# Fifteen block products instead of eleven for the first MLP product of the last two chunks, and last stores on two queues

## The chip, the cores and the metric

The kernel runs on one core of one Trainium2 chip. The metric is the device time of one execution in microseconds, lower is better. Before the change the median of three runs is 528.09 us (527.87 to 530.99).

## What is computed

Eight-head delta-rule attention over a sequence of 768 tokens in four batches, followed by one MLP block with a residual. The reference, cut:

```python
k_n = k / (norm(k) + 1e-6)                      # q, k, v: (4, 8, 768, 48)
for t in range(768):                            # state: (4, 8, 48, 48)
    y[t]  = q[t] @ state
    state = state + beta[t] * outer(k_n[t], v[t] - k_n[t] @ state)
x   = y with heads side by side                 # (4, 768, 384)
xn  = (x - mean) / sqrt(var + 1e-6) * g_ln
out = x + relu(xn @ w_ch1) @ w_ch2              # 384 -> 1536 -> 384
```

Everything is float32. One float32 matmul is two TensorE instructions in the profile.

## The kernel before

**Chunks.** The sequence is cut into 12 chunks of 64 tokens; with four batches a chunk is 256 tokens wide. `recur(c)` carries the delta-rule state from chunk to chunk (small matmuls into the PSUM tiles `two` and `by`, sums on DVE, copies on ACT) and ends in the layer norm. From chunk 3 on the normed tile is transposed on DVE, written to DRAM (`xld`) and read back turned, and ACT multiplies it by the gain into `xnt` (line 1377), three blocks of 128 features. Then `mlp(c)` runs: it is what fills TensorE beside the recurrence of later chunks. The recurrence is ahead of the MLPs: that of chunk 11 has ended when the MLP of chunk 10 begins.

**First product, `eleven` (line 1451).** It forms the hidden layer, 1536 x 256, from `w1_sb` as 2 x 3 blocks (768 x 128) and `xnt` as 3 x 2 blocks (128 x 128), by a scheme of eleven block products in place of twelve. A block product is 6 matmuls of 128x128 weights by 128 columns, so a chunk has 66 matmuls, 132 instructions, all at line 1492. They need sums of token blocks (`d_`, five GpSimd sums per chunk, line 1472) and sums of weight blocks, which `sums_of_w1` (line 1447) makes once, two of them in place in `w1_sb`. The block products accumulate in the four PSUM banks `f0` to `f3`; ACT (lines 1509, 1512) and DVE (lines 1515, 1528) combine them into `h_all`, in two groups with 512 and 256 columns per operation.

**Second product, `seven` (line 1642).** Seven block products of 6 matmuls with 192 columns each (line 1664), with GpSimd forming sums and differences of `h_all` (lines 1650, 1689) and DVE and GpSimd adding up the output tiles `os_` (line 1682). `put(c, g)` stores an output tile with two DMAs (line 600), one for each batch, all on SP's queue. In the last chunk `put(11, 1)` comes first and `put(11, 0)` last.

**Order.** Nothing is issued as it is written down. Each operation is handed to `Line.add` with a cost, and `Line.schedule` plays a list schedule with due times `DUE`, limits `CAP` and one offset `OFF` for each part of the program. `emit` issues in the order of planned starts, and `in_this_order` pins that order on every engine. So a change of a part, or of a number in these lists, moves instructions on all engines; each engine takes its own strictly in order, and a wait at the head holds up all that stands behind it.

Of the kernel before, what the change touches and what calls it, by code (L numbers as in the profile page):

```python
# [16 lines left out]
C = 64  # L17
DP = 64
BK = 32
# [33 lines left out]
def dve(n):  # L53
    return 0.16 + 1.04e-3 * n


def act(n):
    return 0.17 + 0.83e-3 * n
# [371 lines left out]
def kernel(  # L430
# [38 lines left out]
    FROM = 3  # L469
    TOK = 256  # L470
# [6 lines left out]
    def sb(name, shape, dt=FP32):  # L477
        return const.tile(shape, dt, name=name)
# [60 lines left out]
    d_ = [t[:, half_w + 128 * i : half_w + 128 * i + 128] for t in second for i in range(2)] + [ident]  # L539
    st = sb("st", [128, 2, 2, 6])  # L540
# [13 lines left out]
    DUE = [-305.067857599, -184.157488926, 455.196580585, 43.3608971536, 325.931658715, 418.81557092, 734.822875439, 596.087521503, 954.313194593, 1226.15149798, 1753.77174886, 1187.43924725, -1.6924469742, 7.47712706956, 1.31274637377, 1177.34078649]  # L554
    CAP = [747.889715428, 1212.19696458, 1084.81830387, 1850.25080892, 1448.91733639, 908.561376039, 705.970562755, 575.226842462, 821.351411096, 750.46942201, 1687.9172189, 1227.4281115, 847.781737921, 881.489018474, 1102.45793961, 1447.53022967, 1091.57755388]
    T0 = [32.9830988769, 43.9377940451, 29.0921020937, 44.9281472705, 63.7206388166, 107.721780452, 109.01717894, 42.4201425188, 137.327678312, 9.9371017997, 7.55135349446, 21.1072922972, 47.3695615515, 3.2653345546, 12.003557196, 58.3820362978, 9.11313409582, 34.3183793157, 80.7294725245, 31.0940483985, 65.2240956281, 73.1210354066, 26.5270080195, 53.6799046277, 66.9289646085, 120.165225966]
    OFF = [-61.6829581914, -49.2365532767, -61.5532218662, 17.9216944294, -8.93066007944, -19.7935657519, -0.868007026628, 0, 8.96654600389, -13.8380038365, -50.331393939, -0.246849623501, -27.4676130541, 7.77550058171, -22.6886143688, -3.86879544818, -821.586638896, -2.38324144815, -18.1419009006, 5.55478119707, -0.273775179226, -4.22332705522, 80.7687098368, -5.39747372829, -20.4523790178, 62.9055142488, -7.43344176114, 31.9790263038, 21.8074958819, 8.7032008021, 8.84329072182, -13.4908722439, -14.3458640854, -21.0142536144, -8.17343430205, -9.08488196034, 3.21270803936, 29.7501729987, -370.210698155, 9.64783740174, -54.0771745917, 0, 6.02876528764, -18.715620035, -0.0266946289401, -157.574112514, 0.282239804554, -7.26929256528, -11.082495992, -8.27251668698, 6.02892269239, -13.9072145046, 0.152204562562, 22.7850900002, -47.5224937959, -1.16466857269, 2.33155240109, -49.6486518684, -51.2601416133, -62.465549245, -258.793504219, 1.2326483113, 35.4487428898, 31.3088385871, 11.2699410861, -113.147994473, 15.6085619425, -5.03125681565, -202.178096924, -25.0752772067, -0.665071753919, -6.77933533358, 3.23511675889, -68.4395072164, -60.5873923385, -42.4358792875, -97.9842212258, 12.0160900273, 18.6777945201, -900.573997296, -391.422008629, -20.8554491287, 12.9662458348, 1.75202460465, -24.9412070649, 4.97794129872, 75.9129714421, 9.69658805447, 5.43644995158, -526.886362328, -23.7620747742, 4.87077107518, 20.8620167161, 22.9095302211, -1.446032994, -2.31148664706, -2.833545276, 55.9003753723, 63.1638387207, -218.31594106, 287.768221191, 39.9673797514, 0, 804.43668455, 12.7893706811, 40.0678037528, 191.615596099, 0, 7.62314549532, 0, 51.2829387214, 28.4043993347, -5.30420927608, 18.5190140875, -7.64728420003, 7.63987656771, 61.2399462693, 717.489554984, 104.850886777, -30.443334038, -17.6796729001, 1.15630637025, 33.0836625929, 44.5914396091, 124.896962022, 76.2257084997, -17.2048186859, 9.19876963592, 11.8954016929, 17.6790867831, 26.5462796852, 8.59903556167, 24.5744786777, 48.2415672492, 84.1439987925, 573.112593574, -0.31404467451, 2.58380493428, 8.06139582684, -33.4691328586, -35.9526386931, -3.41549753963, 12.8997354829, -1.70472339012, -86.5639462817, 30.2317600188, 0.770084801705, 4.89412762855, 18.4175254922, -4.62459749441, -11.6877931109, 15.5755669109, -4.74496253875, 7.29402960805, -3.92469752656, -16.6201385477, -20.5867367042, 28.2665321084, 4.92853485667, 0, 15.3621971178, -8.42832996846, -56.587083905, 4.72501651567, -56.0564350712, -36.0703739182, 29.6200097296, 32.9003356762, -13.8377451749, 27.2835896047, -1.24739066499, 8.93640941449, 3.28676443186, 297.478212758, -19.9986109974, 45.0956057028, 0, -23.0001510965, 0, 36.6024183436, -9.30579353749, 11.8322652961, 15.1603515043, -21.1764521199, -3.23342658561, 10.9691701204, 0, -53.330288128, -6.9355981517, 35.7517193679, 17.1361544279, -16.5818223692, 7.98946302238, -5.9600414049, 135.238583305, 43.2173490845, 35.7070773331, 1504.57932506, -1.37439939367, 2.80197877523, 83.3684246786, -142.866519066, -50.2056045983, 97.2746589799, 0.00958371475404, 1.62790837443, -2.01014429694, 1.24356061286, 12.6149232043, -4.38744746062, -11.0164345418, -23.3392998149, -60.6068970653, -10.8042936204, -38.5434794118, 2.00080739243, -2.74074762392, -5.2820291742, -29.0236507323, 43.1273234385, 0.946905692554, -24.3700937813, 0, -21.7407793415, -12.5188513858, -23.5560537382, -50.7954370929, -3.45193559535, 15.4383131463, -11.5511037154, 16.3023360558, -25.1832177565, 16.2211956562, 10.4191918731]
# [22 lines left out]
    def half(e):  # L580
        return slice(C * e, C * e + C)
# [837 lines left out]
    def due(c, t):  # L1419
        return DUE[c] + DUE[12 + min(c, 2)] * t  # L1420
# [9 lines left out]
    def w1_part(i, k):  # L1430
        return w1_sb[:, k, i * half_w : i * half_w + half_w], [("w1", k, i, n) for n in range(2)]
# [109 lines left out]

    def mlp(c):
# [5 lines left out]
        if c >= FROM:  # L1548
            hs = [(c * FT + f) % NH for f in range(FT)]
            if c == FROM:  # L1550
                sums_of_w1(True)
            eleven(c, hs)
            return seven(c, hs, 33 * 0.43)
# [43 lines left out]
    def o_keys(g):  # L1597
        return [("o", g, n) for n in range(2)]

    def put(c, g):  # L1600
        line.part += 1
        for e in range(2):
            dma(
                "SP", out[2 * e + g, c * C : (c + 1) * C, :], os_[g][half(e)], C, 105, o_keys(g), [("out", c, g, e)], pr=-5
            )
# [36 lines left out]
    def seven(c, hs, t1=1.3 * FT):  # L1642
# [35 lines left out]
        def sum_(eng, out_, a, b_, r, w, pr=-5):  # L1678
            e = {"Pool": nc.gpsimd, "DVE": nc.vector}[eng]
            add(  # L1680
                eng, dve(D2) if eng == "DVE" else 0.1 + 2.27e-3 * D2,
                lambda: e.tensor_tensor(out=out_, in0=a, in1=b_, op=ALU.add), r, w, pr=pr,  # L1682
            )
# [27 lines left out]
        sum_("Pool", o[1][0], o[1][0], v2, ["v2"], [("o", 1, 0)])  # L1711
# [180 lines left out]
```

## Time and profile before

| what | value |
|---|---|
| median of three runs | 528.09 us |
| profiled execution, own time | 528.0 us |
| span of the profile, first to last instruction | 526.1 us |
| PE busy | 497.6 us (95%), 9706 instructions |
| DVE / ACT / POOL busy | 369.0 / 188.2 / 212.6 us (70 / 36 / 40%) |
| DMA | 40.53 MB, mean 77 GB/s |

The own time of the profiled execution is 1.9 us more than its span; a sum made on the trace is made against 528.0 us. Busy time of PE counts a matmul until its result is there; since matmuls are pipelined, two neighbours overlap, and the distance of two starts says what one costs, not its length.

### The profile page before, as it was taken

What the parts mean: (1) busy time and instruction counts of PE and PEld (TensorE: products, weight loads), DVE (VectorE), ACT (ScalarE), POOL (GpSimd) and SP (SyncE); (2) the same over time, 40 slices, a digit from 0 to 9 for tenths busy, and PEclk for the clock granted to TensorE, in tenths of its full rate; (3) what the DMA queues carried; (4) which work ended last, traced back from release to release, by engine and by line L of the source; (5) the groups of instructions that cost most, each with busy time, mean ns of one, the idle gap of its engine ahead of it and who ended that gap; (6) DMA issues with size and microseconds to landing.
All of it is one profiled execution on the core that took longest, in us unless ns stands there. A gap on an engine that the chain in (4) does not pass through costs nothing.

```text
span 526.1 us, 22198 instructions
## 1 busy us (share of the span) xinstructions
PE 497.6 (95%) x9706; PEld 451.6 (86%) x9706; DVE 369.0 (70%) x849; ACT 188.2 (36%) x420; POOL 212.6 (40%) x320
## 2 busy tenths in 40 slices
PE   6867699999999999999999999999999999999996
PEld 3656577778898999989999889999889999999995
DVE  2899569997399866879895579895678893452321
ACT  2824855414612523525204422513523213242030
POOL 6151432246424560642724342452351815235352
PEclk8776889999999999999999999999999999999999
DMA  9975544365645444454311525121233010221101
GB/s 160 283 138 123 83 133 138 91 103 82 81 70 82 83 90 77 100 80 116 49 31 19 99 55 94 48 61 33 65 64 92 1 32 4 64 68 24 31 2 31
DMA packets 157457, 40.53 MB, mean 77 GB/s; under 512 B 150816, under 2 KB 153888, under 8 KB 157360
## 3 DMA queue, kind: packets, MB, share of 16 engines
q1 hardware_dynamic: 153520, 29.40, 31.3%
q10 hardware_dynamic: 3552, 9.63, 5.8%
q8 instruction: 76, 1.25, 1.0%
q0 software_dynamic: 288, 0.07, 0.2%
q14 instruction: 21, 0.17, 0.1%
HBM read 30.82 MB, written 8.26 MB: 74 GB/s over the span
## 4 chain that ended last, share of the span: by engine, by line
PE 85%; DVE 7%; issue 2%; DMA 2%; POOL 1%; SPq 1%; ACT 0%; DVEq 0%; ACTq 0%
PE f L1664 27%; PE f L1492 25%; PE f L1561 10%; PE two L1256 4%; PE f L1583 3%; PE two L1217 2%; PE by L1217 2%; PE by L1271 2%; PE two L1018 2%; PE two L1281 2%; PE by L1018 1%; DMA kr<-in_k_dram 1%; DVE tmp L1089 1%; PE f L1141 1%; DVE xb L1096 1%
## 5 line engine op out<-in xcount | busy, mean ns | idle before, releaser
L1650 POOL TENSOR_TENSOR h_all<-h_all 128x256 f32<-128x256 f32 x99 | 73.7, 749 | 78.1 <-PE f L1664 65.2
L1664 PE MATMUL f<-w_sb,h_all 128*128 128x192 f32 x396 | 97.2, 334 | 0.9 <-issue 0.5
L1664 PE MATMUL f<-words,h_all 128*128 128x192 f32 x396 | 90.1, 329 | 0.0
L1492 PE MATMUL f<-xnt,w_sb 128*128 128x128 f32 x648 | 87.1, 277 | 0.4 <-ACT xnt L1377 0.3
L1492 PEld LDWEIGHTS f<-xnt,w_sb 128*128 128x128 f32 x648 | 80.0, 192 | 1.6 <-ACT xnt L1377 0.9
L1664 PEld LDWEIGHTS f<-w_sb,h_all 128*128 128x128 f32 x396 | 66.3, 190 | 4.8 <-issue 2.4
L1515 DVE TENSOR_TENSOR h_all<-f,h_all 128x512 f32<-128x512 f32 (+1 forms) x90 | 49.5, 555 | 28.6 <-PE f L1492 19.4
L1689 POOL TENSOR_TENSOR words<-h_all 128x128 f32<-128x128 f32 x66 | 34.2, 537 | 85.8 <-ACT h_all L1512 77.7
L1664 PEld LDWEIGHTS f<-words,h_all 128*128 128x128 f32 x396 | 67.6, 190 | 1.1 <-ACT xln L1336 0.2
L1179 DVE TENSOR_TENSOR tmp<-xb,gb 128x31 f32<-128x31 f32 (+15 forms) x155 | 62.4, 403 | 5.5 <-POOL xb L1165 1.4
L1186 DVE TENSOR_TENSOR xb<-xb,tmp 128x31 f32<-128x31 f32 (+15 forms) x155 | 59.7, 385 | 4.0
L1561 PE MATMUL f<-xnt,w_sb 128*128 128x256 f32 x216 | 54.3, 397 | 2.0 <-issue 2.0
L1561 PEld LDWEIGHTS f<-xnt,w_sb 128*128 128x128 f32 x216 | 41.3, 196 | 8.9 <-issue 2.3
L1266 ACT COPY u<-two 128x768 f32<-128x768 f32 x24 | 19.2, 799 | 51.2 <-PE two L1256 44.1
L1492 PE MATMUL f<-second,w_sb 128*128 128x128 f32 x216 | 33.1, 276 | 1.0 <-POOL second L1472 1.0
L1512 ACT ACTIVATE h_all<-f 128x512 f32<-128x512 f32 (+1 forms) x36 | 17.4, 490 | 43.6 <-PE f L1492 31.6
L1682 DVE TENSOR_TENSOR o<-f,x 128x192 f32<-128x192 f32 x33 | 11.6, 353 | 30.0 <-PE f L1664 17.1
L1570 ACT ACTIVATE h_all<-f 128x256 f32<-128x256 f32 x36 | 13.8, 383 | 52.2 <-PE f L1561 52.0
L1664 PE MATMUL f<-w_sb,words 128*128 128x192 f32 x132 | 32.1, 328 | 0.0
L1492 PEld LDWEIGHTS f<-second,w_sb 128*128 128x128 f32 x216 | 29.2, 192 | 1.4 <-POOL second L1472 1.3
L1512 ACT ACTIVATE h_all<-h_all 128x512 f32<-128x512 f32 (+1 forms) x36 | 18.8, 521 | 30.2 <-DVE h_all L1515 30.1
L877 DVE STREAM_TRANSPOSE kq<-tb 128x256 f32<-128x256 f32 (+2 forms) x34 | 23.9, 725 | 2.1 <-PE two L1217 1.1
(194 smaller groups left out, 831.7 us busy)
## 6 DMA issues: line engine op xcount, KB each, us to landing
words<-in_moe_w_ch_dram ACTq DMA_DIRECT2D x8, 768.0 KB
out_dram<-o SPq DMA_DIRECT2D x48, 96.0 KB
xld<-xlt SPq DMA_DIRECT2D x9, 384.0 KB
xnt<-xld SPq DMA_DIRECT2D x36, 96.0 KB
tb<-in_q_dram SPq DMA_DIRECT2D x40, 64.0 KB
tb<-in_k_dram SPq DMA_DIRECT2D x32, 64.0 KB
v<-in_v_dram SPq DMA_DIRECT2D x8, 192.0 KB
w_sb<-in_moe_w_ch_dram ACTq DMA_DIRECT2D x2, 768.0 KB
```

The lines of the kernel that those rows point to most:

```text
L877: "DVE", 0.18 + 1.035e-3 * n, lambda o=o, w=w: nc.vector.transpose(o, w), tb_keys(i, "blk"),
L1179: lambda j=j, n=n, w=w, t=t: nc.vector.tensor_tensor(out=t, in0=xb[:, 0:n, j : j + 1].to_broadcast([128, n, w]), in1=gb[:, j : j + 1, j + ...
L1186: "DVE", dve(n * w), lambda t=t, rest=rest: nc.vector.tensor_tensor(out=rest, in0=rest, in1=t, op=ALU.subtract),
L1217: nc.tensor.matmul(dst[half(e), hp, j], src[drows(hp), (e if n else key_half(c, hp, e)) * GP + j], s_all[drows(hp), e, j], start=(n == 0 o ...
L1256: nc.tensor.matmul(*args(e, e ^ hp, 2 * (j + NP * g) + hp))
L1492: nc.tensor.matmul(wide(p[:, o : o + 128]), w[:, f : f + 128], r, start=start and m == n == 0, stop=stop, skip_group_check=True)
L1512: add("ACT", act(128 * m), lambda: nc.scalar.activation(to[0], p, ACTF.Relu), pk, to[1])
L1515: add("DVE", dve(128 * m), lambda v=ps(p): nc.vector.tensor_tensor(out=to[0], in0=v, in1=y[0], op=op), [*pk, *y[1]], to[1])
L1561: nc.tensor.matmul(p[:, 0:TOK], w1_sb[:, t, f * 128 : (f + 1) * 128], xnt[:, t], start=(t == 0), stop=(t == KC - 1))
L1650: add(eng, cost, lambda: e.tensor_tensor(out=out_, in0=x, in1=y, op=op), r, w, port=2 if eng == "Pool" else 1, pr=-2)
L1664: lambda f=f, t=start and f == 0: nc.tensor.matmul(p[:, 0:D2], lhs(f), rhs[:, f], start=t, stop=(f == F2 - 1), skip_group_check=True),
L1689: lambda f=f + i: e.tensor_tensor(out=s3[f], in0=one(0, 0)[0](f), in1=one(1, 0)[0](f), op=ALU.subtract),
```

## The change

For chunks 10 and 11 (`c >= LAST`) the first product is formed by `fifteen`: `w1_sb` as 3 x 3 blocks (512 x 128), `xnt` as 3 x 2 blocks, fifteen block products of 4 matmuls each. It needs eleven token sums per chunk on GpSimd (`e_`, in the two `second` tiles), six weight blocks made from the originals into the query and key buffers `tb` (`r_`, nine GpSimd sums), six DVE edits of `w1_sb` in place and two negations on ACT. Before that `thirds_of_w1` undoes the two in-place sums of `sums_of_w1` with four DVE subtractions. All outputs of a block product are combined in one group of 512 columns.

In the last chunk one of the two stores of each output tile goes to ACT's queue, and the sum into `o[1][0]` moves from GpSimd to DVE. Three numbers of `DUE` and some of `OFF` differ, and `seven` takes its PSUM banks in another order in chunks 10 and 11. The issue order on every engine is the same as before until late in the program: the first difference on GpSimd is in the MLP of chunk 8, on the others in that of chunk 9.

```diff
+    LAST = 10
...
+    OW = DFF // 3
+    r_ = [t[:, OW * i : OW * i + OW] for t in tb for i in range(2)]
+    e_ = [t[:, 128 * i : 128 * i + 128] for t in second for i in range(6)]
...
+    def W(k, o):
+        return w1_sb[:, k, OW * o : OW * o + OW], [("w1", k, (o + n) // 2, (o + n) % 2) for n in range(2)]
...
+    def thirds_of_w1():
...
+        for i in range(2):
+            (o, ok), (a, ak) = w1_part(1 - i, i), w1_part(1 - i, 1 - i)
+            for n in range(2):
+                f = slice(384 * n, 384 * n + 384)
+                add("DVE", dve(384), ... o[:, f] = o[:, f] - a[:, f] ...)
+        for (o, ok), (a, ak), (b, bk), op in (
+            (R(5), W(0, 0), W(2, 0), ALU.add), (R(5), R(5), W(2, 1), ALU.subtract),
+            (R(0), W(1, 2), W(0, 1), ALU.subtract), (R(1), W(1, 0), W(2, 1), ALU.subtract), (R(2), W(0, 0), W(2, 2), ALU.subtract),
+            (R(3), W(0, 0), W(0, 2), ALU.add), (R(3), R(3), W(1, 2), ALU.subtract),
+            (R(4), W(1, 2), W(1, 1), ALU.subtract), (R(4), R(4), W(2, 1), ALU.add),
+            (W(2, 0), W(1, 0), W(2, 0), ALU.subtract), (W(2, 0), W(2, 0), W(2, 2), ALU.subtract),
+            (W(0, 2), W(0, 1), W(0, 2), ALU.subtract), (W(0, 2), W(0, 2), W(2, 2), ALU.subtract),
+            (W(1, 1), W(0, 1), W(1, 1), ALU.subtract), (W(1, 1), W(1, 1), W(1, 0), ALU.add),
+        ):
+            # in place in w1: DVE; into r_: GpSimd, after the last load of tb was used
...
+        for o, ok in (W(1, 2), W(1, 0)):
+            add("ACT", act(OW), lambda o=o: nc.scalar.mul(o, o, -1.0), [], ok)
+
+    def fifteen(c, hs):
...
+        M = 4
+        def prod(p, pk, r, w, start=False):      # 4 matmuls, two to a step
...
+        prod(pa, ka, D(0), W(0, 1), True)
+        copy(h(1, 1), pa, ka)
+        prod(pb, kb, D(1), W(2, 1), True)
+        copy(h(0, 1), pb, kb)
+        prod(pc, kc, D(2), W(2, 2), True)
+        copy(h(0, 0), pc, kc)
+        sum_(h(0, 1), pc, kc)
+        prod(pd, kd, X(1, 2), R(5), True)
+        copy(h(1, 0), pd, kd)
+        prod(pa, ka, D(3), R(0))
+        sum_(h(0, 1), pa, ka, ALU.subtract)
+        prod(pb, kb, D(4), R(1))
+        sum_(h(0, 0), pb, kb)
+        prod(pd, kd, D(5), W(2, 0))
+        sum_(h(0, 0), pd, kd, ALU.subtract)
+        prod(pc, kc, D(6), W(1, 2))
+        copy(h(0, 2), pc, kc)
+        prod(pa, ka, X(0, 0), W(0, 2))
+        sum_(h(1, 0), pa, ka)
+        sum_(h(0, 2), pa, ka)
+        relu(h(0, 2), -1.0)
+        prod(pb, kb, D(7), W(1, 0))
+        sum_(h(1, 0), pb, kb, ALU.subtract)
+        prod(pc, kc, X(0, 1), R(4))
+        sum_(h(0, 1), pc, kc, ALU.subtract)
+        relu(h(0, 1))
+        prod(pa, ka, D(8), W(0, 0))
+        sum_(h(1, 0), pa, ka, ALU.subtract)
+        relu(h(1, 0))
+        prod(pd, kd, D(9), R(2), True)
+        sum_(h(0, 0), pd, kd)
+        relu(h(0, 0))
+        copy(h(1, 2), pd, kd)
+        prod(pb, kb, X(1, 1), W(1, 1))
+        sum_(h(1, 1), pb, kb, ALU.subtract)
+        relu(h(1, 1))
+        prod(pa, ka, D(10), R(3))
+        sum_(h(1, 2), pa, ka, ALU.subtract, first=1)
+        relu(h(1, 2))
...
     def mlp(c):
-            eleven(c, hs)
-            return seven(c, hs, 33 * 0.43)
+            if c == LAST:
+                thirds_of_w1()
+            if c < LAST:
+                eleven(c, hs)
+                return seven(c, hs, 33 * 0.43)
+            fifteen(c, hs)
+            return seven(c, hs, 30 * 0.43)
...
     def put(c, g):
-                "SP", out[2 * e + g, ...
+                "ACT" if e and c == NCH - 1 else "SP", out[2 * e + g, ...
...
     def seven(c, hs, t1=1.3 * FT):
-            (pa, ka), (pb, kb), (pc, kc) = (fours[(turns[2] + i) % 4] for i in (3, 0, 1))
-            turns[2] += 2
+            order = (3, 0, 1) if c < LAST else (3, 2, 1) if (c - LAST) % 2 == 0 else (1, 2, 3)
+            (pa, ka), (pb, kb), (pc, kc) = (fours[(turns[2] + i) % 4] for i in order)
+            turns[2] += 2 * (c < LAST)
...
-        sum_("Pool", o[1][0], o[1][0], v2, ["v2"], [("o", 1, 0)])
+        near = "DVE" if c == NCH - 1 else "Pool"
+        sum_(near, o[1][0], o[1][0], v2, ["v2"], [("o", 1, 0)])
```

The names used below: a *third sum* is one of the nine GpSimd sums into `r_`, an *edit* one of the DVE operations on `w1_sb`, a *token sum* one of the GpSimd sums into `e_`.

More of the change, by code (lines that the diff above doesn't have):

```diff
@@ L552 @@
     xld = dram.tile([128, KC, 4, 2 * BK], FP32, name="xld")
-    DUE = [-305.067857599, -184.157488926, 455.196580585, 43.3608971536, 325.931658715, 418.81557092, 734.822875439, 596.087521503, 954.313194593, 1226.15149798, 1753.77174886, 1187.43924725, -1.6924469742, 7.47712706956, 1.31274637377, 1177.34078649]
+    DUE = [-305.067857599, -184.157488926, 455.196580585, 43.3608971536, 325.931658715, 418.81557092, 734.822875439, 596.087521503, 954.313194593, 3397.14759519, 2128.20730596, 1906.59705915, -1.6924469742, 7.47712706956, 1.31274637377, 1177.34078649]
@@ L1603, in put @@
             dma(
-                "SP", out[2 * e + g, c * C : (c + 1) * C, :], os_[g][half(e)], C, 105, o_keys(g), [("out", c, g, e)], pr=-5
+                "ACT" if e and c == NCH - 1 else "SP", out[2 * e + g, c * C : (c + 1) * C, :], os_[g][half(e)], C, 105, o_keys(g), [("out", c, g, e)], pr=-5
             )
```

57 lines of the change are left out of this document (56 added, 1 removed).

## The prediction

> **What bounds the kernel now.** I read the page first, then the chain that ended last for the part the change touches, then windows of it.
>
> ```profile
> span 526.1 us, 22198 instructions
> PE 497.6 (95%) x9706; PEld 451.6 (86%) x9706; DVE 369.0 (70%) x849; ACT 188.2 (36%) x420; POOL 212.6 (40%) x320
> PE   6867699999999999999999999999999999999996
> POOL 6151432246424560642724342452351815235352
> PEclk8776889999999999999999999999999999999999
> ```
>
> From the seventh slice on TensorE is full, at full granted clock. The chain from 425 us on (start, length, what) consists of TensorE alone up to 521.3 us:
>
> ```profile
> 465.01 13.40 PE f L1492 x120
> ...
> 480.16 7.48 PE f L1664 x46
> ...
> 493.40 13.40 PE f L1492 x120
> ...
> 507.57 13.71 PE f L1664 x82
> ...
> 521.37 0.36 DVE o L1682
> ```
>
> The two stretches of 120 instructions are chunk 10's and chunk 11's first product. One instruction costs 13.40/120 = 0.1117 us there, and one of the second product 7.48/46 = 0.1626 us. The groups show a mean length of 277 ns instead, which is the time to the result; neighbours overlap, so it would mislead as a price:
>
> ```profile
> L1492 PE MATMUL f<-xnt,w_sb 128*128 128x128 f32 x648 | 87.1, 277 | 0.4 <-ACT xnt L1377 0.3
> ```
>
> What the other engines do in the touched stretch (length, then PE, PEld, DVE, ACT and POOL busy, granted clock, DMA):
>
> ```profile
> 425.00:441.00 16.00, 16.00 (x309) 15.57 (x308) 12.13 (x26) 4.50 (x9) 3.11 (x6) 1.00 0.09 22
> 441.00:463.20 22.20, 22.20 (x657) 19.83 (x656) 7.81 (x18) 7.09 (x15) 7.96 (x13) 1.00 0.14 40
> 463.20:478.50 15.30, 15.30 (x135) 15.30 (x135) 8.15 (x19) 5.57 (x13) 3.33 (x8) 1.00 0.29 78
> 492.50:507.50 15.00, 15.00 (x134) 15.00 (x133) 7.16 (x14) 4.31 (x9) 4.23 (x8) 1.00 0.11 27
> ```
>
> So time is won here only by fewer TensorE instructions, and lost where one of them waits. The rest is the tail after the last matmul, about 5 us.
>
> **Part 1: the block products.** Instructions of line 1492 in both first products (busy is behind the length):
>
> ```profile
> 463.00:507.60 44.60, 30.87 (x264) 30.46 (x264) 1.00 0.14 36
> ```
>
> 264 in two chunks, 132 in each, which is 11 x 6 matmuls x 2. Fifteen products of 4 matmuls are 120. Shape, clock and operand layout stay, so 24 instructions go: 24 x 0.1117 = **-2.68 us**. It all lies on the path. The small chunk-by-chunk shifts of order before that move no instruction count on TensorE; I give them nothing, covered by TensorE's full queue.
>
> **Part 2: the weights between chunks 9 and 10.** Everything in `thirds_of_w1` is added work on DVE, GpSimd and ACT. The trace has no sum of 128x512 from SBUF on GpSimd; the nearest rows are one of the timeline (start, length) and groups (count, busy, mean ns, idle before):
>
> ```profile
> 480.22 1.28 POOL L1689 TENSOR_TENSOR words<-h_all 128x128 f32<-128x128 f32 x3
> L1650 POOL TENSOR_TENSOR h_all<-h_all 128x256 f32<-128x256 f32 x99 | 73.7, 749 | 78.1 <-PE f L1664 65.2 <-ACT h_all L1570 9.8 <-DMA kr<-in_k_dram 0.7
> L857 POOL TENSOR_TENSOR v<-v,knrms 128x768 f32<-128x768 f32 x10 | 15.5, 1548 | 23.3 <-PE f L1492 9.4 <-PE f L1561 7.0 <-DMA v<-in_v_dram 4.6
> L1447 POOL TENSOR_TENSOR w_sb<-w_sb 128x384 f32<-128x384 f32 x4 | 4.8, 1208 | 2.2 <-PE f L1561 2.2
> L1515 DVE TENSOR_TENSOR h_all<-f,h_all 128x512 f32<-128x512 f32 x45 | 30.9, 686 | 19.1 <-PE f L1492 13.5 <-ACT h_all L1509 4.5
> ```
>
> Midway between 0.75 (256) and 1.55 (768) a third sum is 1.15 us; at the slow rate of the 384 row, 1.208 x 512/384 = 1.61. Three of the nine stand earlier in GpSimd's order, in chunk 8's MLP near 363 us, a slice with POOL at two tenths: 3.5 us of idle engine. Six, 6.9 us, stand between chunk 9's sums; GpSimd is idle 14.2 of the 22.2 us before 463.2. DVE gets four undo steps (384 columns, about 0.55 each by the 512 row) and six edits of 0.69: 6.3 us against 14.4 idle. ACT gets two negations, taken at DVE's 0.69, against 15.1 idle.
>
> What counts is who stands behind a waiting edit. In DVE's order the first two edits of 512 columns wait for third sums that still read the old columns, and behind them stand the sum of chunk 9's output, the state update of chunk 10 and chunk 11's `v` sum, which TensorE's recurrence waits for. GpSimd can start once the first undo is through. That stands in DVE's order just ahead of this pair, in the idle time shown, so at about 435.1 us; it then has three third sums, four differences of 128 columns (1.28/3 = 0.43 each) and two sums of 256 (0.75) to do: 3 x 1.15 + 3.2 = 6.7 us, to 441.8. Two edits in sequence, 1.4 us, end at 443.2; the state update is next due where it runs now (start, length):
>
> ```profile
> 435.12 0.95 DVE L1515 TENSOR_TENSOR h_all<-f,h_all 128x256 f32<-128x256 f32 x2 [0.96 <-ACT h_all L1509]
> ...
> 445.69 0.95 DVE L1291 TENSOR_TENSOR s_all<-s_all,two 112x768 f32<-112x768 f32 x1 [5.29 <-PE two L1281]
> ```
>
> That leaves over 2 us. At 1.61 per third sum the edits end at 444.6, still ahead of it. I take **0**; below nothing isn't possible. If the cover is gone (2.2 us a third sum, edits of twice the time) they end at 447.7 (435.1 + 6.6 + 3.2 + 2.8), and TensorE, which goes on with the recurrence only after the state update, loses 2.0 us: that end is kept for the range.
>
> In a sentence beside this: the Trainium skill's page "SBUF — State Buffer", section "SBUF: two separate sides", has a GpSimd sum and a DVE operation with two SBUF inputs lock each other out for a whole instruction, which speaks against weight edits on both engines at once. The 1208 against 749 ns above is the kind of lengthening it would explain. By it an edit waits for at most one third sum, so that the first pair would end at most 1.15 later, near 444.4, and the sum stays as it is; it adds to the chance of rival A.
>
> **Part 3: the first product of chunk 10 begins.** Now (start, length, engine; PE is in instructions, two to a matmul):
>
> ```profile
> 460.60 1.15 PE L1271 MATMUL by<-u,pt 64*64 64x48 f32 x64
> 461.68 1.57 PE L1664 MATMUL f<-w_sb,h_all 128*128 128x192 f32 x8
> 461.87 0.48 ACT L1312 COPY x<-by 128x384 f32<-128x384 f32 x1 [1.86 <-PE by L1271]
> 462.24 1.30 ACT L1377 ACTIVATE xnt<-xnt,g_sb 128x256 f32<-128x256 f32 x3
> 463.20 0.71 PE L1492 MATMUL f<-xnt,w_sb 128*128 128x128 f32 x4
> ```
>
> The first product wants the scaled `xnt`, and ACT does that behind its copy of chunk 11's `by`. Between `by` and the first product stand 4 matmuls, 461.68 + 8 x 0.1626 = 462.98; it starts at 463.20, a wait of some 0.2 already. After the change ACT has both copies ahead of the three `xnt` steps, and TensorE begins with a product of the third step. Copies lie 0.37 apart: 461.87 + 2 x 0.37 + 1.30 = 463.91. TensorE has 6 second-product matmuls first: 461.68 + 12 x 0.1626 = 463.63. The wait is 0.28 to 0.33 in place of 0.2: **+0.1 us**. The token sums (128 columns, as the 0.43 us differences) come faster than the 0.89 us in which TensorE uses one.
>
> **Part 4: banks.** A block product is 8 x 0.1117 = 0.89 us, and its bank is free when DVE has taken it. Counted from the start of its last instruction: 0.28 to the result, 0.1 to DVE (as from the last matmul at 521.27 to the sum at 521.37), 0.69 for the sum and at most 0.1 back, 1.17 us. Two other products in between give 0.11 + 1.79 = 1.90, which covers it by 0.7, or by one more DVE sum ahead in the queue. There are now 12 sums of 512 columns a chunk, 8.3 us, where DVE is busy for 7.16 us in all of 492.5 to 507.5 now. In TensorE's order the one place with less cover is the end of chunk 11: between the products with `D(8)` and `D(10)`, on one bank, stands a single product, 1.00 us, so 0.17 is lost. Chunk 10 has a second-product matmul there as well (0.33) and loses nothing. **+0.2 us**, from 0 to 0.9 (another sum in front).
>
> **Part 5: the tail.** Now:
>
> ```profile
> 518.30 0.81 PE L1664 MATMUL f<-w_sb,words 128*128 128x192 f32 x4
> 519.08 2.19 PE L1664 MATMUL f<-w_sb,h_all 128*128 128x192 f32 x12
> 519.15 0.36 DVE L1682 TENSOR_TENSOR words<-f,words 128x192 f32<-128x192 f32 x1 [0.22 <-PE f L1664]
> 519.59 1.13 POOL L1682 TENSOR_TENSOR o<-o,words 128x192 f32<-128x192 f32 x2 [3.10 <-DVE words L1682]
> 520.75 2.39 SPq L600 DMA_DIRECT2D out_dram<-o  x4
> L600 SPq DMA_DIRECT2D out_dram<-o x2: 547/572/598, 522.0 to 522.5; - x2
> DMA  0000006997149961399813998200000000000000
> ```
>
> The last row has forty slices from 521.1 to 526.1 us, 0.125 each: four bursts of some 0.6 us, one per store, the last ending near 524.4. Let T be the end of the last matmul, 521.27. The last store is issued at 522.5 = T+1.28, its data ends at T+3.13. No store runs on ACT's queue in this trace; I take SP's times for it. After the change the product that feeds `words` ends 2 matmuls before T instead of 6, so `words` is summed at T-0.2, and both halves of `o[1]` (DVE 0.36, GpSimd 0.58) and the last sum of `o[0]` end near T+0.45. All four stores are then issued in two pairs, at T+0.5 and T+1.05. One burst follows its issue by 1.1 us (520.75 to the first nonzero slice, 521.85). If two bursts run at once without loss, the end is T+1.05+1.1+0.6 = T+2.75, 0.4 won. If they share what one uses now (slices at 9), four bursts of 0.6 follow each other from T+1.6 to T+4.0, 0.9 lost. The 20 nonzero slices average six tenths, so four bursts packed without a gap take 20 x 0.125 x 0.61 = 1.5 us, to T+3.1; they will not pack so well, and I take T+3.3, between the ends: **+0.2 us**.
>
> **Sum.** 528.0 - 2.68 + 0 + 0.1 + 0.2 + 0.2 = 525.8 on the profiled execution. It lies 0.1 under the median shown (528.09), so **525.9 us**, 0.4% less. A measurement of this kernel can tell about 1% from no change.
>
> **Rivals.**
> A. *The edits hold up DVE's queue.* Place: the state update of chunk 10 behind the first two edits. For it: in-order queue, six third sums between chunk 9's own GpSimd work, the 1208 ns row. Against it: 2 us of cover. Price up to 2.0, so 525.9 + 2.0 = 527.9 in full, 526.9 for half of it.
> B. *Slower: TensorE waits for banks.* There are no longer two groups of outputs to take turns; 11 products a chunk reuse a bank, 22 in all. From the point where a drain meets two sums ahead of it on DVE, each reuse loses 2 x 0.69 - 0.73 = 0.65 us. If a third of them do, 7 x 0.65 = 4.6: 525.9 + 4.6 = 530.5 us, if two thirds, 535. For it: twelve long sums a chunk, some of them two to a product. Against it: DVE does nothing else then, and its 8.3 us are spread over 13.4.
> C. *The two queues do not disturb each other, and the late `words` costs nothing.* The tail gives 0.4 rather than taking 0.2: 525.3 us. For it: the bursts leave slices at 1 between them; against: slices at 9 within.
> D. *The saving is not there*, since TensorE is bound by weight loads rather than instruction count: 528.5 us with the added waits. Against it: starts lie an even 0.1117 apart, and there is one load per matmul instruction before (x9706 for both on the page) as after.
>
> **How the numbers follow.** Forecast 0.64, A 0.11, B 0.10, C 0.13, D 0.02. The forecast's own range is 525.2 to 526.6. The range given goes from 525.0 (-2.68, no waits, the tail's best, 0.38, on 528.09) to 528.4 (A in full, the bank wait at 0.9); past it are B and D in part, under 2 in 10. Faster by over 1% would need 522.8, more than all removed instructions: 0.01. Slower by over 1% (533.4) is B nearly in full: 0.04. Within 1%: 0.95.
>
> **What would show it.** Right: 240 first-product instructions in the two chunks at 0.112 us, twice 13.4 us and little between; TensorE's last matmul near 519.0 us; the state update of chunk 10 within 0.5 us of 445.7; about 0.3 us of wait before the first product of chunk 10 and about 0.2 before the last of chunk 11. In the tail four bursts packed from T+1.6, ending near T+3.3. Wrong: gaps between first-product matmuls released by DVE (B), a DVE edit that ends after 445.7 (A), a last matmul no earlier than 521 (D), a tail that ends by T+2.8 (C) or past T+4.

## The result and the profile after

The changed kernel takes 526.83 us (median of 13 executions, 524.70 to 529.47) against 530.46 us for the kernel before in the same executions (13, 527.87 to 532.72): a ratio of 0.9943, 95% interval 0.9920 to 0.9965. That is 0.57% less, 0.35 to 0.80. The forecast was 525.9 on a before of 528.09, 0.42% less. The kernel before ran some 2 us slower in the later executions than in the three first shown, so the ratio is the number to compare. In time it is 3.0 us of 530.46, with an interval from 1.9 to 4.2.

The page of the profiled execution first:

```profile
span 527.2 us, 22200 instructions
PE 497.4 (94%) x9682; PEld 451.7 (86%) x9682; DVE 380.5 (72%) x860; ACT 193.5 (37%) x426; POOL 230.6 (44%) x340
PEclk8576789999999999999999999999999999999999
```

The span is longer than before (526.1), although TensorE has 24 instructions fewer (9706 before) and its clock is full from the seventh slice on in both. So the difference must be looked for by place. Take a matmul that has as many TensorE instructions ahead of it in both kernels, the first of line 1260 (1256 before) in chunk 10's recurrence: it starts at 434.34 us in the kernel before and at 437.65 here, so this execution is 3.3 us late before an instruction is saved. From that matmul to the end of the last one (the expectations below call it "from chunk 9's first recurrence matmul"; it is chunk 10's), the windows (length, PE, PEld, DVE, ACT and POOL busy, clock, DMA share, GB/s) of the kernel before,

```profile
434.34:521.27 86.93, 86.93 (x1316) 83.53 (x1316) 30.49 (x67) 23.03 (x49) 36.13 (x64) 1.00 0.11 29
```

and of the changed kernel, the second row for line 1612 alone,

```profile
437.65:522.11 84.46, 84.25 (x1292) 80.89 (x1292) 41.38 (x79) 28.67 (x55) 49.54 (x81) 1.00 0.11 30
463.00:513.00 50.00, 28.91 (x240) 28.21 (x240) 1.00 0.13 33
```

show the change: 86.93 us became 84.46, **2.47 less**, with 24 instructions fewer; DVE got 10.9 us of work more, GpSimd 13.4, ACT 5.6. The tail after the last matmul went from 4.8 to 5.1 us (527.2 - 522.11). Together 2.2 us less, inside the interval of 1.9 to 4.2.

Where the weights are rearranged (the timeline of GpSimd and DVE; start, length):

```profile
437.83 0.55 DVE L1559 TENSOR_TENSOR w_sb<-w_sb 128x384 f32<-128x384 f32 x1
438.46 1.28 POOL L1573 TENSOR_TENSOR tb<-w_sb 128x512 f32<-128x512 f32 x1 [11.70 <-DVE w_sb L1559]
...
443.60 2.81 POOL L1573 TENSOR_TENSOR tb<-w_sb 128x512 f32<-128x512 f32 x2
446.45 1.79 DVE L1573 TENSOR_TENSOR w_sb<-w_sb 128x512 f32<-128x512 f32 x2 [1.97 <-POOL tb L1573]
448.16 0.35 DVE L1823 TENSOR_TENSOR o<-f,x 128x192 f32<-128x192 f32 x1
448.88 0.95 DVE L1295 TENSOR_TENSOR s_all<-s_all,two 112x768 f32<-112x768 f32 x1 [0.37 <-PE two L1285]
```

The two edits wait 1.97 us for GpSimd, and behind them the state update still waits 0.37 us for TensorE: it is in time. Then chunk 10's first product begins,

```profile
465.11 0.86 ACT L1316 COPY x<-by 128x384 f32<-128x384 f32 x2 [1.81 <-PE by L1275]
465.85 1.31 ACT L1381 ACTIVATE xnt<-xnt,g_sb 128x256 f32<-128x256 f32 x3
465.99 1.14 PE L1805 MATMUL f<-w_sb,words 128*128 128x192 f32 x6
467.22 0.71 PE L1612 MATMUL f<-xnt,tb 128*128 128x128 f32 x4
```

which waits for the third `xnt` step: six instructions at 0.1626 end at 465.99 + 0.98 = 466.97, and the product starts at 467.22, 0.25 later. The end of chunk 11's first product is the one place where TensorE waits for a PSUM bank:

```profile
505.76 2.03 DVE L1631 TENSOR_TENSOR h_all<-h_all,f 128x512 f32<-128x512 f32 x3 [0.44 <-PE f L1612]
506.01 1.06 PE L1612 MATMUL f<-xnt,w_sb 128*128 128x128 f32 x8
507.19 0.68 PE L1612 MATMUL f<-second,tb 128*128 128x128 f32 x4
```

Eight instructions at 0.1117 end at 506.90; the next starts at 507.19. That it is the bank follows from DVE's second sum in the first row, which empties it and ends at 507.05, and from `sums_longer` below, where the wait at this place grows with the DVE sums and is put down to them. And the tail, with the busy share of the DMA engines in forty slices of 0.125 us from 522.0:

```profile
521.50 0.36 DVE L1823 TENSOR_TENSOR words<-f,words 128x192 f32<-128x192 f32 x1 [2.96 <-PE f L1805]
521.89 0.36 DVE L1823 TENSOR_TENSOR o<-o,words 128x192 f32<-128x192 f32 x1
521.94 0.76 POOL L1823 TENSOR_TENSOR o<-o,words 128x192 f32<-128x192 f32 x1 [3.38 <-DVE words L1823]
522.22 0.36 DVE L1823 TENSOR_TENSOR o<-f,o 128x192 f32<-128x192 f32 x1
522.73 1.11 SPq L604 DMA_DIRECT2D out_dram<-o  x2
522.73 1.38 ACTq L604 DMA_DIRECT2D out_dram<-o  x2
```

```profile
DMA  0000000000000028997999979930000000000000
```

`words` is ready only 0.25 us before the last matmul's end (T = 522.11), so all four stores leave after T, and the data run from T+1.64 to about T+3.4 (a slice under a tenth follows the last digit shown).

### The profile page after: what moved, and what is told of

It is laid out like the page before. It is cut to its first block, busy times and chain, and to the rows that moved or that the text cites. A ratio compares the mean times of both kernels' runs of the same rounds, so it can differ in the third digit from the quotient of the medians.

```text
span 527.2 us, 22200 instructions
## 1 busy us (share of the span) xinstructions
PE 497.4 (94%) x9682; PEld 451.7 (86%) x9682; DVE 380.5 (72%) x860; ACT 193.5 (37%) x426; POOL 230.6 (44%) x340
## 4 chain that ended last, share of the span: by engine, by line
PE 77%; DVE 6%; DMA 4%; issue 4%; ACT 2%; POOL 2%; SPq 2%; POOLq 0%; DVEq 0%; ACTq 0%
PE f L1805 22%; PE f L1496 18%; PE f L1701 10%; PE two L1260 5%; PE f L1612 5%; PE f L1723 3%; PE by L1221 2%; PE by L1275 2%; PE two L1221 2%; DMA kr<-in_k_dram 2%; SPq L604 2%; PE two L1285 2%; PE two L1022 1%; POOL h_all L1790 1%; DMA xnt<-xld 1%
## 5 line engine op out<-in xcount | busy, mean ns | idle before, releaser
L1790 POOL TENSOR_TENSOR h_all<-h_all 128x256 f32<-128x256 f32 x99 | 75.3, 768 | 62.0 <-PE f L1805 48.6
L1496 PE MATMUL f<-xnt,w_sb 128*128 128x128 f32 x504 | 67.7, 277 | 0.4 <-ACT xnt L1381 0.3
L1183 DVE TENSOR_TENSOR tmp<-xb,gb 128x31 f32<-128x31 f32 (+15 forms) x155 | 60.6, 391 | 4.4 <-POOL xb L1169 0.2
L1496 PEld LDWEIGHTS f<-xnt,w_sb 128*128 128x128 f32 x504 | 62.1, 192 | 1.3 <-ACT xnt L1381 0.6
L1519 DVE TENSOR_TENSOR h_all<-f,h_all 128x512 f32<-128x512 f32 (+1 forms) x70 | 38.4, 554 | 15.7 <-PE f L1496 9.5
L1701 PEld LDWEIGHTS f<-xnt,w_sb 128*128 128x128 f32 x216 | 41.2, 196 | 7.8 <-issue 1.2
L1516 ACT ACTIVATE h_all<-f 128x512 f32<-128x512 f32 (+1 forms) x28 | 13.5, 490 | 39.8 <-PE f L1496 24.0
L1496 PE MATMUL f<-second,w_sb 128*128 128x128 f32 x168 | 25.8, 276 | 2.4 <-POOL second L1476 2.4
L861 POOL TENSOR_TENSOR v<-v,knrms 128x768 f32<-128x768 f32 x10 | 15.3, 1529 | 25.9 <-DMA v<-in_v_dram 10.1
L1496 PEld LDWEIGHTS f<-second,w_sb 128*128 128x128 f32 x168 | 22.8, 192 | 2.7 <-POOL second L1476 2.7
```

The costliest lines, as they stand in the source:

```text
L1183: lambda j=j, n=n, w=w, t=t: nc.vector.tensor_tensor(out=t, in0=xb[:, 0:n, j : j + 1].to_broadcast([128, n, w]), in1=gb[:, j : j + 1, j + ...
L1496: nc.tensor.matmul(wide(p[:, o : o + 128]), w[:, f : f + 128], r, start=start and m == n == 0, stop=stop, skip_group_check=True)
L1519: add("DVE", dve(128 * m), lambda v=ps(p): nc.vector.tensor_tensor(out=to[0], in0=v, in1=y[0], op=op), [*pk, *y[1]], to[1])
L1701: nc.tensor.matmul(p[:, 0:TOK], w1_sb[:, t, f * 128 : (f + 1) * 128], xnt[:, t], start=(t == 0), stop=(t == KC - 1))
L1790: add(eng, cost, lambda: e.tensor_tensor(out=out_, in0=x, in1=y, op=op), r, w, port=2 if eng == "Pool" else 1, pr=-2)
```

## The experiments

My theory was the prediction's own account, with three parts worth testing: the gain is the instruction count and nothing else; the weight work is free, but by how much; the tail has a gain (two queues) and a loss (late `words`) of about one size. The rivals were A (the edits delay the state update), B (banks) and that the 3.3 us of delay belong to the change, since three third sums do stand earlier, at 357 to 370 us (chunk 7's MLP by count; the prediction says chunk 8's).

**changed_again.** No edit.

> The changed kernel once more. Theory: the 3.3 us that its first profile was late before the changed stretch are that execution's own and not the change's, so that the last matmul stands near 519.0 us (2.3 before that of the kernel before), the stretch from chunk 9's first recurrence matmul to it takes 84.5 us and the tail 5.1; ratio to before 0.9943 within 0.002. Rival (the early third sums in chunk 8's stretch cost 1.1 us): TensorE again falls back by about 1 us between 367 and 397.

Ratio 0.9941 (0.9916 to 0.9966). The windows:

```profile
436.05:520.84 84.79, 84.52 (x1292) 80.97 (x1292) 41.48 (x79) 28.68 (x55) 49.44 (x81) 1.00 0.11 30
```

The stretch is 84.79 us, 0.22 of it one stall (a gap before a matmul that the profile puts down to no releaser) inside a product; the tail 525.9 - 520.84 = 5.1. This execution comes to the stretch 1.7 us late, not 3.3, and between 355 and 397 us its TensorE falls back by under 0.1 us. In the first profile 2.2 of the 3.3 us are there before the first third sum starts (the matmul at 333.9 us in the kernel before starts at 336.1), so they can't be the third sums'. For the other 1.1, the early third sums cost nothing in this execution; in the other eight profiles of the changed order TensorE falls back by between -0.1 and 1.1 us over these instructions, in a second execution of the order before (`tail_on_before`) by 0.1. A cost of a few tenths there is not ruled out. What differs ahead of the stretch differs from execution to execution: the nine others with as many TensorE instructions ahead of it reach it between 434.0 and 441.7 us. My 519.0 for the last matmul was missed here, as in the first profile, for that reason.

**thirds_small.** In `thirds_of_w1` and only there:

```diff
-o[:, f], in0=o[:, f], in1=a[:, f]          # undo, DVE
+o[:, f][:, 0:8], in0=o[:, f][:, 0:8], in1=a[:, f][:, 0:8]
-e.tensor_tensor(out=o, in0=a, in1=b, op=op)   # third sums and edits
+e.tensor_tensor(out=o[:, 0:8], in0=a[:, 0:8], in1=b[:, 0:8], op=op)
-nc.scalar.mul(o, o, -1.0)
+nc.scalar.mul(o[:, 0:8], o[:, 0:8], -1.0)
```

> The changed kernel with every third sum, edit, undo step and negation of the weights cut to 8 columns: the same instructions in the same order with the same waits, each as short as it can be (the weights of the last two chunks are then not the ones the products need). Theory (part 2 costs nothing): from chunk 9's first recurrence matmul to the last matmul 84.5 us as in the changed kernel (up to 0.4 more where TensorE's issue stalls). Rival A (the edits hold up DVE's queue): 1 to 2 us shorter. The same is asked of the stretch of chunk 8, where three third sums stand: no shift of TensorE between 367 and 397 us against the kernel before.

```profile
441.66:526.44 84.78, 84.53 (x1292) 80.97 (x1292) 34.85 (x79) 27.81 (x55) 40.62 (x80) 1.00 0.11 30
```

84.78 us, 0.2 of it again a stall inside a product: no gain from taking 6.5 us off DVE and 8.9 off GpSimd. Rival A falls: in this stretch the weight work costs TensorE nothing. The other half of the expectation was not met in its words, since TensorE did shift by 0.9 us between 355 and 397; but here the sums there are as short as can be, so their length isn't the reason.

**thirds_twice.** Line 1573 issues each operation twice.

```diff
-e.tensor_tensor(out=o, in0=a, in1=b, op=op)
+[e.tensor_tensor(out=o, in0=a, in1=b, op=op) for _ in range(2)]
```

> The changed kernel with each third sum and each edit of line 1573 done twice (weights again not the right ones). This takes the cover away on purpose: three third sums of 1.3 us and two edits of 0.7 more stand ahead of chunk 10's state update. Theory (in-order queue with some 0.1 to 0.5 us of cover left in the changed kernel): the update comes 5 us later and TensorE, which cannot go on with the recurrence without it, loses 4 to 5 us; the stretch to the last matmul grows from 84.5 to about 89. Rival (the work is hidden by a wide margin, as a cover of over 5 us would have it): 84.5 again.

The stretch, and in it the wait and what follows (windows, then the sum of TensorE's waits):

```profile
440.99:533.55 92.56, 87.54 (x1292) 83.36 (x1292) 47.80 (x85) 28.57 (x55) 59.37 (x87) 0.96 0.10 27
453.00:458.10 5.10, 0.54 (x5) 0.24 (x2) 4.29 (x6) 0.86 (x2) 5.02 (x6) 0.93 0.00 0
458.10:464.50 6.40, 6.34 (x79) 5.84 (x80) 4.61 (x10) 1.82 (x5) 6.24 (x6) 0.53 0.01 3
```

```profile
PE f L1805 <- DVE o L1823: 4.8, 2, 4.6
```

```profile
453.70 4.05 DVE L1573 TENSOR_TENSOR w_sb<-w_sb 128x512 f32<-128x512 f32 x4 [5.88 <-POOL tb L1573]
457.67 0.34 DVE L1823 TENSOR_TENSOR o<-f,x 128x192 f32<-128x192 f32 x1
```

The edits now wait 5.88 us for GpSimd's third sums. The wait on TensorE is as expected in size, but not in place: what TensorE waits for is the bank that DVE's sum of chunk 9's output empties, one instruction ahead of the state update. That sum starts 16.7 us into the stretch here (457.67 - 440.99) against 10.5 in the changed kernel (448.16 - 437.65): 6.2 us later for 4.8 lost, a cover of 1.4 us (the time by which it may come later before TensorE waits). And the price is 8.1 us, not 4 to 5. After the wait TensorE's granted clock is 0.53 over 6.4 us, which costs another 3. The Trainium skill's page "TensorE: Matmul & The Clock Gate", section "What's actually happening", has the clock halved after an idle window of about 3.4 us; the 4.6 us wait here agrees, and the waits of 0.3 us in the changed kernel bring no such row.

**last11.** Fifteen products in chunk 11 alone.

```diff
-    LAST = 10
+    LAST = 11
```

> Fifteen products in chunk 11 alone, chunk 10 with eleven; the weight edits come one chunk later. Theory (the saving is the instruction count): line 1496 and line 1612 together 252 instructions in the two first products, 12 fewer than before, so 1.34 us off the stretch to the last matmul, less some 0.3 of waits: half of what the full change takes off (2.47). Ratio to before about 0.997. Rival (the saving comes from the new plan numbers, or one chunk pays for the edits): no gain or a loss against before, ratio 1.000 or more.

Ratio 0.9973 (0.9941 to 1.0005).

```profile
435.45:521.95 86.50, 85.95 (x1304) 82.05 (x1304) 40.64 (x79) 26.13 (x53) 48.41 (x75) 1.00 0.11 29
```

```profile
458.85 0.40 PE L1260 MATMUL two<-v,xt 32*32 32x48 f32 x32 [0.35 <-issue]
...
490.03 0.52 PEld L1612 LDWEIGHTS f<-second,w_sb 128*128 128x128 f32 x4 [0.37 <-POOL second L1600]
```

Twelve instructions fewer, but only 0.43 us of 1.34 (86.50 against 86.93), where some 1.0 was expected. Three waits take the rest: 0.25 before the first of the fifteen (on GpSimd's token sums), 0.29 before the last, as in the changed kernel, and 0.35 of stall in the recurrence: -1.34 + 0.89 = -0.45. The price per instruction holds; what waits add is of its own size and doesn't shrink with it. The ratio's interval reaches past 1, so the times alone don't rule out the rival of no gain; it is the one stretch that speaks against it.

**last9.** Fifteen products in three chunks.

```diff
-    LAST = 10
+    LAST = 9
```

> Fifteen products in chunks 9, 10 and 11; the weight edits come one chunk earlier, where DVE also does the 256-column row sums of the last inverse. Theory (instruction count): 12 instructions fewer again, a further 1.34 us off, ratio to before about 0.992 at best. Rival A (the edits hold up DVE's queue): in chunk 8's stretch DVE has its cover taken by the row sums, the state update of chunk 9 comes late and TensorE loses 1 to 4 us there, which eats the 1.34 or more: ratio 0.994 to 1.000. Rival B (bank waits): gaps before first-product matmuls of chunk 9, released by DVE.

**last9_small.** The same with the 8-column weight work of thirds_small.

> Fifteen products in chunks 9, 10 and 11, with third sums, edits, undo steps and negations cut to 8 columns as in thirds_small (TensorE's order is that of last9). last9 lost 15.5 us. Theory (the length of the weight work did it: third sums of 1.3 to 1.7 us stand ahead of the token sums on GpSimd, the first product of chunk 9 waits, and the granted clock falls behind the later waits): most of the loss goes, and time comes to within 3 us of the kernel before. Rival (the order that the plan gives TensorE there, the recurrence of chunk 10 behind the whole first product of chunk 9, costs it whatever the edits take): at least 10 us of the loss stay.

last9 is slower: ratio 1.0319 (1.0261 to 1.0377). From the same matmul at the start of chunk 8's first product to the last one, 123.76 us in the kernel before, it takes 141.66; the second row is where most is lost:

```profile
398.68:540.34 141.66, 128.54 (x1572) 122.98 (x1570) 79.40 (x147) 38.84 (x75) 68.54 (x110) 0.92 0.11 28
...
466.00:483.00 17.00, 8.38 (x374) 7.34 (x374) 5.03 (x14) 5.43 (x11) 1.47 (x4) 0.54 0.23 61
```

and last9_small, with its chain at the same place:

```profile
399.78:535.80 136.02, 125.30 (x1572) 120.29 (x1570) 71.21 (x147) 37.71 (x75) 57.95 (x109) 0.94 0.11 29
```

```profile
451.14 0.73 PE two L1260 x51
...
467.11 4.63 DMA xld<-xlt
474.76 2.67 DMA xnt<-xld
```

The small weight work gives back 5.6 of 17.9 us. The other 12.3 stay, though no edit of any length is left to wait for: the rival was right. With `LAST = 9` chunk 10's recurrence stands behind the whole first product of chunk 9 (at 451 us here, at 437.65 in the changed kernel, inside that product), so the way from the recurrence over the layer norm and its round trip through DRAM to `xnt` lies bare, with little other TensorE work beside it; in last9 TensorE is busy 8.4 of 17 us there and gets 0.54 of its clock. The 5.6 us that the weight work does cost in last9 are not rival A as it was worded, a state update late behind DVE's edits. They begin on GpSimd, where four third sums in a row (420.36 to 426.28 us) stand ahead of chunk 9's token sums, for which its first product waits:

```profile
PE f L1612 <- POOL second L1600: 1.9, 2, 1.4
```

Rival B's waits are small: DVE holds up first-product matmuls by 1.0 us in all. The plan's numbers for chunk 9 there are those set for eleven products; whether others would bring three chunks home wasn't tried.

**sums_longer.** In `fifteen`:

```diff
-nc.vector.tensor_tensor(out=to[0], in0=v[first], in1=v[1 - first], op=op)
+[nc.vector.tensor_tensor(out=to[0][:, :k], in0=v[first][:, :k], in1=v[1 - first][:, :k], op=op) for k in (2, 4)]
```

> The changed kernel with one change to its twelve DVE sums a chunk: half of each sum is done twice (the hidden values are then not the right ones), so that a sum holds DVE for about 1.1 us in place of 0.69 and the twelve for 13 of the 13.4 us of a chunk's block products. Theory (a bank is free in time as long as no drain meets a second one in DVE's queue; cover 0.7 us): the waits before chunk 11's last product grows from 0.29 to about 0.7, and a few others appear where a product has two sums; 1 to 4 us in all over the two chunks. Rival B as predicted (each of 22 reuses loses what the sums lack of cover): 22 x 0.4 = 9 us or more. If the sums of the changed kernel had no cover at all, gaps would stand before nearly every product already.

```profile
PE f L1612 <- DVE h_all L1631: 3.7, 4, 1.8
PE f L1805 <- DVE h_all L1631: 0.7, 1, 0.7
```

```profile
502.77 8.52 DVE L1631 TENSOR_TENSOR h_all<-h_all,f 128x256 f32<-128x256 f32 x16 [1.52 <-PE f L1612]
```

The stretch takes 90.6 us, 6.2 more, between my 1 to 4 and the rival's 9; 4.4 of it are waits by the profile, the rest wasn't taken apart. The rival had the shape wrong: there are five waits, not 22 small ones. The theory had few waits right, but not their size: the last is 1.8 us, not 0.7, because DVE's queue has piled up by then. Sixteen DVE instructions (eight sums) run without a gap for 8.52 us, 1.07 a sum against 0.89 for a product, and two of the waits, 1.09 and 1.81, fall into this run. In the changed kernel a sum takes 0.69, less than a product, and the queue holds TensorE up only at the last product.

**one_queue.** The stores all on SP and the near sum of `o[1]` on GpSimd, as in the kernel before.

```diff
-"ACT" if e and c == NCH - 1 else "SP", out[...]
+"SP", out[...]
-near = "DVE" if c == NCH - 1 else "Pool"
+near = "Pool"
```

> The changed kernel with only its tail undone: all four last stores on SP's queue and the near sum of o[1] on GpSimd again. Theory: the last matmul stays where the change puts it, T; the two GpSimd sums of o[1] follow each other to about T+1.0, the stores leave SP one behind the other, about 0.6 us each, from T+0.6 to T+2.3, and the last data land near T+4.0. The tail after T is about 5.7 us in place of 5.1 changed and 4.8 before; time 0.6 us above the changed kernel, ratio to before about 0.995 to 0.996. Rival (the second queue brings nothing, the engines that carry the data are the limit): tail 5.1 as changed.

**tail_on_before.** The kernel before, with half of the last stores on ACT's queue.

```diff
-"SP", out[...]
+"ACT" if e and c == NCH - 1 else "SP", out[...]
```

> The kernel before with nothing changed but the queue of two of its last four stores (ACT in place of SP). Theory: o[1]'s pair leaves at once on both queues before T, o[0]'s pair at about T+0.6 in place of T+0.7 and T+1.3; the tail after the last matmul goes from 4.84 to about 4.2 us, the rest stays. Rival (a store's own start-up sets the end, not its place in a queue): tail 4.7 or more.

**words_first.** The last product waits, in the plan alone, for the one that feeds `words`:

```diff
-        prod(pb, kb, *one(0, 1), *b(1, 1), start=False)
+        prod(pb, kb, *one(0, 1), b(1, 1)[0], lambda f: b(1, 1)[1](f) + (kc if c == NCH - 1 else []), start=False)
```

> The changed kernel with the words product of chunk 11 finished 6 matmuls before the last one instead of 2 (its order on TensorE alone changes, same instructions). Theory: the last matmul T stays; words is summed by T-0.5, both halves of o[1] by T+0.1, so the first two stores leave at about T+0.2, one on each queue, and their data are through before the second pair (issued near T+0.6) needs the engines: last data at about T+2.8 in place of T+3.4, 0.6 us less. Rival (start-up of a store and not sharing sets the end): last data within 0.2 of T+3.4.

one_queue (ratio 0.9960, 0.9925 to 0.9995), with its last sums and stores; its stretch has one stall of 0.35 us:

```profile
434.00:518.92 84.92, 84.52 (x1292) 80.97 (x1292) 41.23 (x78) 28.67 (x55) 49.39 (x81) 1.00 0.11 30
```

```profile
518.74 1.13 POOL L1823 TENSOR_TENSOR o<-o,words 128x192 f32<-128x192 f32 x2 [3.38 <-DVE words L1823]
519.41 2.39 SPq L604 DMA_DIRECT2D out_dram<-o  x4
```

tail_on_before, where the last matmul ends at 522.40 and the span at 526.6; its stretch is a second measurement of the order before, 86.96 us against 86.93:

```profile
435.44:522.40 86.96, 86.93 (x1316) 83.53 (x1316) 30.50 (x67) 23.04 (x49) 36.24 (x64) 1.00 0.11 29
```

```profile
521.88 1.47 SPq L600 DMA_DIRECT2D out_dram<-o  x2
521.89 1.51 ACTq L600 DMA_DIRECT2D out_dram<-o  x2
```

words_first (ratio 0.9919, 0.9887 to 0.9950), with the DMA slices from 519.0 us:

```profile
434.70:519.19 84.49, 84.28 (x1292) 80.94 (x1292) 41.50 (x79) 28.64 (x55) 50.05 (x81) 1.00 0.11 30
```

```profile
518.50 1.65 SPq L604 DMA_DIRECT2D out_dram<-o  x2
518.51 1.69 ACTq L604 DMA_DIRECT2D out_dram<-o  x2
```

```profile
DMA  0000069999920039989940000000000000000000
```

The tail after the last matmul, span less its end, in one table:

| | `words` early | `words` late |
|---|---|---|
| one queue | 4.8 (before) | 5.9 (one_queue) |
| two queues | 4.2 (tail_on_before, words_first) | 5.1 (changed) |

The second queue brings 0.6 to 0.8 us either way; the late `words` costs 0.9 (two queues) to 1.1 (one). The near sum of `o[1]` is on GpSimd in the row of one queue and in tail_on_before, on DVE in the others, so the 0.8 holds the queue and that sum together. The tail hardly differs between executions: five more profiles with the changed tail (`changed_again`, `thirds_small`, `thirds_twice`, `sums_longer`, `last11`) have 5.1 too. In words_first the first pair's data are through by T+1.3 and the second's by T+2.55, with T = 519.19, where the changed kernel packs all four up to T+3.4. My T+2.8 was 0.25 too late.

**words_first_again**, beside changed_again.

> words_first once more beside the changed kernel on one chip. Theory: the same last matmul and a tail 0.9 us shorter, ratio to before about 0.0017 below the changed kernel's. Rival: no difference between the two.

Ratio 0.9895 (0.9843 to 0.9946) against changed_again's 0.9941; the last matmul ends at 518.63, the span at 522.8, again 4.2 of tail. The two intervals of each pair overlap, so the times alone only suggest the difference; the tail shows it, 4.2 to 5.1 in two executions each. This version is ahead of the kernel before by its ratio, and of the changed one by its tail.

## Why the prediction was right

The forecast case came true; the time lies 0.9 us above it, inside its range, and the ratio's interval (0.35% to 0.80% less) holds the 0.42%. That the time itself lands in the range owes something to the later executions being slower: by the ratio, 528.09 would have become 525.1, just above the range's lower end of 525.0. The mechanism is borne out in the stretch and the tail, whose 2.2 us are those of the forecast. (The upper end, 528.4, leaves the tail's +0.2 out of its sum; with it, 528.6.)

- *Part 1*, -2.68 us: 240 instructions, 0.1117 apart. Of 2.68 us, 2.47 arrived in the stretch; Parts 3 and 4 were to take 0.3 of it. Their two waits are there, and by the prediction's count they add 0.03 and 0.29; about 0.1 came back elsewhere, since the gap of 0.13 us before the last twelve instructions of the kernel before (518.30 + 4 x 0.1626 = 518.95 against 519.08) has gone with the new order. The stretch of words_first (84.49) bears the price out, and last11 does once its waits are counted. One sign of rival D came up in the first profile, a last matmul no earlier than 521 (522.11), through the 3.3 us ahead of the stretch; D is out all the same, since the stretch is shorter by what the instructions cost. That the two first products take "twice 13.4 us" is only true of their instructions: second-product matmuls stand among them.
- *Part 2*, 0: right, and shown by thirds_small. But the term that was to keep it so, a cover of over 2 us from the edits to the state update, was mis-sized: the update would have been late after 0.37 (its result is ready at 449.83, and TensorE's next use of it starts at 450.77, 0.94 later). So the 0 came true with less to spare than claimed. On the clock of the kernel before (3.31 us back) GpSimd's first third sum came at 435.15, as worked out; its third one ended at 443.1 in place of 441.8, since a third sum took 1.28 to 1.40 instead of 1.15 and the sums between them 3.9 (439.74 to 443.60) instead of 3.2; the edits took 1.79 instead of 1.4 and ended at 444.9; and the sum of chunk 9's output, named as standing behind them but left out of the working, took 0.35 more. That sum, not the update, is what TensorE meets first when the edits are late, and thirds_twice puts the cover there at 1.4 us. The price "if the cover is gone", 2.0, was for a milder case, but it left out the clock, which adds 3 us to a 4.8 us wait.
- The Trainium skill's page "SBUF — State Buffer", section "SBUF: two separate sides", gave the prediction its later end of the pair, near 444.4; it came at 444.9. The trace agrees with the lock in size: in the changed kernel's timeline,

```profile
453.31 1.83 DVE L1573 TENSOR_TENSOR w_sb<-w_sb 128x512 f32<-128x512 f32 x1
453.33 1.26 POOL L1573 TENSOR_TENSOR tb<-tb,w_sb 128x512 f32<-128x512 f32 x1
...
456.02 0.64 DVE L1573 TENSOR_TENSOR w_sb<-w_sb 128x512 f32<-128x512 f32 x1
```

  an edit that began with a third sum took 1.83 us, one without 0.64: about one third sum (1.26) more. Which of the two held the other can't be read from starts 0.02 us apart; the third sum had its usual length.
- *Part 3*, a wait of 0.28 to 0.33: 0.25. *Part 4*, 0.17 to 0.2 at one place: 0.29 at that place and no other. It is 0.1 longer than forecast: the DVE sum that empties the bank started only at 506.37, behind another sum that ran until 506.45 (neighbours on DVE overlap a little in the profile). Rival B begins somewhere between a DVE sum of 0.69 us and one of 1.07, longer than a block product (0.89), as sums_longer shows.
- *Part 5*, +0.2: +0.25. The stores left at T+0.62 (0.5 forecast), because GpSimd's half took 0.76 rather than 0.58; data from T+1.64 (1.6) to T+3.4 (3.3). Rival C was half right: two queues do save 0.6 us, over its 0.4, but the late `words`, which it took as free, costs more than that.
- The last matmul near 519.0 us: 522.1, 520.8, 519.2, 518.9 and 518.6 us in five executions with as many instructions up to it. What a single profile shows ahead of the changed stretch must be taken off first.

## What to carry to other kernels

On a full TensorE an instruction removed was worth its spacing and no more; look for the rest in what the edit adds at its borders, here a first product that starts on a later input, a last one that reuses a bank too soon, and the order of the last two products. Work on idle engines was free up to a cover, 1.4 us here, that is found by following what stands behind it in its queue; past it the price can be more than the wait, since the clock was halved after the wait of 4.6 us, though not after waits of up to 1.8 us in sums_longer. Compare two profiles of kernels with one beginning by the instruction, not by the microsecond.

## What was not expected of the hardware

A wait of 4.6 us on TensorE was followed by 6.4 us at 0.53 of its clock, so that 4.8 us of waiting cost 8.1. GpSimd's sums of 256 columns, 0.75 us in the kernel before, took up to 1.17 beside DVE's weight edits and undo steps. TensorE had single stalls of 0.2 to 0.35 us inside a product or the recurrence, released by nothing that the profile shows, in some executions and not in others. Two stores on two queues carried their 192 KB in about 0.9 us, against 0.6 for one of 96 KB alone before.
